# Row results in pieces of rows, and query weights transposed ahead, in a forward-and-backward decode block

## The chip, the cores and the metric

The kernel runs on one core of one Trainium2 chip. A core has a matrix engine (PE), a vector engine (DVE), an activation engine (ACT), a general engine (POOL) and a queue engine (SP) that only issues DMAs; 16 DMA engines move data between the device's memory and the core's on-chip memory (SBUF). PE writes to PSUM, from which DVE and ACT evict. The metric is the device time of one execution in microseconds, lower is better.

## The reference

The block is a sum of two branches on a normalised input, and the kernel computes its output and all gradients for one given `grad_out`:

```python
xn = layernorm(x)                                  # x: 2 x 1 x 576
# A: grouped-query attention on a cache
q = (xn @ wq)                                      # 32 heads of 128, 16 kv heads, 4096 cached rows
p = softmax(q k^T * 128 ** -0.5); o = p v
y = x + (o @ wo) + ((xn @ w_gate) * (xn @ w_up)) @ w_down     # F = 4608
out_0 = y
out_1 .. out_8 = gradients by x, k_cache, v_cache, wq, wo, w_gate, w_up, w_down
```

There are two rows (batch 2, one position each). The caches are 2 x 16 x 4096 x 128 in bf16, 33.6 MB each; their gradients, 33.6 MB each, are outer products of a vector over the cached rows and a vector over the 128 columns. All weights' gradients are outer products of rank two as well. So nearly all of the 186 MB that move are caches and weights read once and gradients written once. `out_0` and `out_1` are two rows of 576 values each. `out_1`, the gradient by x, is `grad_out` plus the layernorm's backward: (xn * mean(xn * g) − g + mean(g)) times −rstd, where g is the gradient by xn, added up over all groups and all MLP slices.

## The kernel before, in words

**Work.** The 16 kv heads are taken in eight groups of two, each for both rows of the batch: 16 steps `s`, group `s // 2`. A step loads two K and two V tiles of 1 MB (`load_kv`, L1132), turns each by two DVE transposes in 32 x 32 blocks (`turn`, L1207), scores on PE, softmax (`softmax`, L1316), the backward of it (`dscore`, L1372), two contractions with K and V (`contract`, L1423), and builds the four 1 MB gradient tiles by outer products on PE that ACT and DVE evict (`head_outer`, L1276, `unit`, L703) and SP stores (`put`, L696). The weights of a group are 0.5 MB of `wq` and 0.58 MB of `wo` (`load_w`, L1150). `group_front` (L982) computes q and the gradient by o; `group_back` (L1048) comes after both steps of a group: it adds the group's part of y to `acc` (L1082) and its part of the gradient by xn to `accx` (L1109), and starts the stores of the weights' gradients. The MLP is nine slices of 512 (`mlp`, L857), each of which adds to `acc` (L939) and `accx` (L971) too.

**Buffers.** All 1 MB tiles share 16 buffers `big` (L414): loaded K and V (`kv`, at most 6), turned tiles (`X`, at most 10), tiles to be stored (`st`, at most 5), gate and up weights (`G`). The weights of groups and slices share five buffers `ww`. For the part of the gradient by xn, `group_back` takes an `X` buffer, turns the group's `wq` into it by two DVE transposes (1.25 and 0.4 us in the planner's costs, L1098 and L1101), and only then gives the `ww` buffer back (L1099); then 32 products (`dxn`, L677) and the addition to `accx`.

**Order.** The engines' instruction streams are fixed when the program is built. Each piece of work is a generator that yields what it needs (an engine for so long, a buffer, an event); the class `Order` (L105) simulates these with its own costs and at each point gives an engine the piece of best priority among those that can start within `SLACK[engine]`. A priority is `STEP * s + PR[name]` plus tables by name and step (`pr`, L350; `OFF`, `HEAD`, `TAIL`); `WQ_AT`, `WO_AT`, `MLP_AT` say after how many K/V loads a weight's load may be issued. All large DMAs are issued by SP, in order; a DMA that waits for its buffer or its data holds up all that come after it on SP.

**Row results.** `consts` (L533) builds small masks. The last part of `front` (L641 to L668) makes x and the layernorm's values in columns: `xnT`, 128 partitions x 16. `acc` holds y as 5 chunks of 128 columns x 2 rows, on 128 partitions; `accx` holds the gradient by xn, folded over partitions, as 144 columns. At the end `final_out` (L1491) waits for all 17 additions to `acc`, turns it into two rows by nine fp32 products and adds x by two more products (`rows_add`, L1486), all into one PSUM tile of two partitions; ACT and DVE each evict a part (`rows_put`, L1478) and one DMA stores the row pair. `final_dx` (L1510) waits for the additions to `accx`, folds it by two products into 16 columns, computes the layernorm's backward in columns with eight small DVE operations and one product for the means, and turns the result into rows by eight fp32 products. In the order before it both have the same priority name, `fin`.

Of the kernel before, what the change touches and what calls it, by code (L numbers as in the profile page):

```python
# [13 lines left out]
P = 128  # L14
# [276 lines left out]
def DMA(engine, cost, nbytes, row=8192):  # L291
# [7 lines left out]
OFF = {"turn0": {0: 171.1, 1: 102.6, 2: -235.3, 3: 131.0, 4: -1229.9, 5: -180.7, 6: 339.1, 7: 83.9, 8: -1178.9, 9:  # L299
       1510.3, 10: 1749.8, 11: 637.8, 12: -214.3, 13: 330.3, 14: -900.9, 15: 113.0}, "turn1": {0: 455.2, 1: 413.9,  # L300
       2: 2138.7, 3: 65.8, 4: -397.2, 5: -528.4, 6: -1010.6, 7: -442.2, 8: -480.8, 9: -56.6, 10: 2098.4, 11: 87.0,
       12: -533.6, 13: -186.7, 14: 1823.6, 15: -1825.2}, "att": {0: -86.1, 1: 484.3, 2: 959.1, 3: 205.8, 4: -477.9,
       5: 588.8, 6: -2779.3, 7: -570.9, 8: 538.0, 9: -432.8, 10: -333.4, 11: 178.6, 12: 1763.9, 13: -38.0, 14: 9.3,
       15: -454.9}, "dsc": {0: -2.6, 1: -25.2, 2: 108.7, 4: -124.6, 5: 280.8, 6: -182.4, 7: 505.0, 8: 999.6, 10:
       1142.0, 12: -1624.8, 13: 450.2, 14: 26.1, 15: -1895.7}, "conv": {0: -1227.4, 1: -997.7, 2: -24.5, 3: 7.4, 4:
       -1788.1, 5: 528.6, 6: -1155.3, 7: -233.7, 8: -14.9, 9: 46.4, 10: -63.6, 11: -273.8, 12: -324.9, 13: -904.4,
       14: 156.5, 15: -1289.5}, "con": {0: 72.5, 1: 1065.5, 2: 2112.7, 3: 144.9, 4: 1119.6, 5: -318.8, 6: -807.3, 7:
# [4 lines left out]
       -906.9, 15: 763.8}, "front": {0: -1381.5, 1: -23.4, 2: -755.9, 3: 528.2, 4: 2459.1, 5: 22.3, 6: 15.4, 7:  # L312
       1614.9, 8: 1.0, 10: 390.9, 11: -4409.0, 12: 71.6, 13: -2214.6, 14: -86.2, 15: -206.6}, "back": {0: -538.7, 1:
# [7 lines left out]
       575.5, 9: -1893.1, 10: 29.8, 11: 1312.5, 12: -1551.8, 13: 2261.8, 14: -58.6, 15: -683.8}, "mlp": {0: 1005.2,  # L321
       1: -119.9, 2: 307.5, 4: -272.5, 5: -538.3, 6: -1285.0, 7: -2206.3, 8: -1506.9, 9: -1373.7, 10: -36.4, 11:
       -236.4, 12: 122.0, 13: 9.3, 14: -2474.7, 15: -1534.6}, "load": {0: 498.6, 1: 724.3, 2: -50.1, 3: 540.2, 4:
       106.4, 5: 1070.9, 6: -4.7, 7: -442.3, 8: 13.7, 9: -963.6, 10: -542.2, 11: -703.0, 12: -151.2, 13: 45.9, 14:
       -640.8}, "wload": {0: 155.4, 1: 205.4, 2: -85.0, 3: -865.8, 4: -2.0, 5: 2.5, 6: -0.9, 7: -303.6, 8: -1673.8,
       9: 962.0, 10: -188.9, 11: -608.2, 12: 86.0, 13: -143.2, 14: 1336.5, 15: 67.0}, "mload": {0: 43.2, 1: -50.8,
       2: 543.7, 3: -706.6, 4: -994.4, 6: -292.2, 8: 4096.0, 9: 58.8, 10: 972.1, 11: -299.2, 12: -233.4, 13: -24.9,
       14: 4269.4, 15: 2.2}}
MLP_AT = [0.0, 18.84, 14.07, 104.31, 26.44, 110.17, 0.0, 165.05, 136.25]
WQ_AT = [-187, 8, 14, 18, -93, -80, 45, 31]  # L330
WO_AT = [-23, -224, -88, -8, 34, 20, -51, -5]
# [3 lines left out]
BIAS = 0.255  # L335
SLACK = {"PE": 0.03, "ACT": 0.26, "DVE": 0.37, "POOL": 10000.0, "SP": 10000.0}
STEP = 28.0
HEAD = {"turn0": 81.5, "turn1": -4923.1, "att": -4504.9, "dsc": 207.7, "conv": -115.1, "con": 711.3, "out1":
        -3897.8, "out0": 1625.0, "front": 7985.6, "back": -1026.0, "W0": 2562.1, "W1": 3202.9, "BD1": -1330.7,
        "BD0": 7636.5, "mlp": 1972.6, "load": -4759.7, "wload": 3596.4, "mload": -2011.8}  # L340
TAIL = {"turn0": 4716.0, "turn1": 3086.8, "att": -169.4, "dsc": 2547.1, "conv": 1801.7, "con": 5805.3, "out1":
        12765.0, "out0": -437.4, "front": -225.5, "back": 3672.3, "W0": 3335.0, "W1": 3885.8, "BD1": -3217.7, "BD0":
        2296.5, "mlp": -2755.5, "load": -1393.2, "wload": 1480.7, "mload": -4914.1}
PR = {"turn0": 1153.7, "turn1": 1076.7, "att": -5721.2, "dsc": -1832.7, "conv": 859.0, "con": -1218.3, "out1":
      5153.5, "out0": 3270.3, "front": 245.1, "back": 420.1, "W0": -4343.9, "W1": 6157.7, "BD1": 4299.8, "BD0":
      -734.7, "mlp": -683.6, "wout": -1070.7, "store": 4212.6, "load": -375.6, "wload": -10719.3, "fin": 6841.0,
      "const": 8800.2, "mload": -3635.3}
# [8 lines left out]
def kernel(  # L356
# [121 lines left out]
    nmu = const.tile([2, 1], FP32, name="nmu")  # L478
    warm = const.tile([1, 1], FP32, name="warm")
    rstd = const.tile([2, 1], FP32, name="rstd")  # L480
# [9 lines left out]
    one1 = filled("one1", [1, 1], FP32, 1.0)  # L490
    ones = filled("ones", [P, 1], FP32, 1.0)
    meanc = filled("meanc", [P, 1], FP32, 1.0 / D)
    xnT = filled("xnT", [P, 16], FP32, 0.0)
    nrT = const.tile([P, 4], FP32, name="nrT")
    gg = const.tile([P, 2, 16], FP32, name="gg")
    gp4 = const.tile([P, 4], FP32, name="gp4")
    zero1 = filled("zero1", [P, 1], FP32, 0.0)
    acc = filled("acc", [P, 5, 2], FP32, 0.0)
# [104 lines left out]
    def front():  # L603
# [52 lines left out]
        for a in range(4):  # L656
            nc.tensor.matmul(tp[0:16, 8 + 2 * a:10 + 2 * a], lhsT=xb[:, 512 + 16 * a:528 + 16 * a],
                             rhs=ident[0:2, 0:2], start=True, stop=True)
# [932 lines left out]
```

## Time and profile before

| | |
|---|---|
| time, median of 3 runs | 467.26 us (466.91 to 468.17) |
| the profiled execution | 468.62 us, of which the span of its instructions 466.8 |
| moved | 185.87 MB in all packets; HBM read 92.48 MB, written 92.48 MB |
| mean rate over the span | 398 GB/s |
| busy | PE 78%, DVE 79%, ACT 70%, POOL 34% |
| mean granted PE clock | 0.72 of full |

The profile's page cuts the span into 40 slices of 11.7 us and gives each engine's busy share in tenths, the granted clock, the DMA engines' share and the rate. Its windows do the same for any stretch; a DMA share a little over 1 means that all sixteen are busy, since a packet's record overlaps the next by a few ns. Lists of waits say for which instruction of which engine an engine stood still, in total, how often and how long at most; `SPq` is SP's queue. The timeline lists instructions by start and duration, with the engine, the line, the operation and the tiles (`ps_m`, `ps_o` are PSUM tiles). fp32 products appear as pairs of instructions.

### The profile page before, as it was taken

Reading aid. Unit: us, or ns where it says so; the run is one execution under the profiler, and the core shown is the slowest. Engines: PE = TensorE matmul, PEld = TensorE weight load, DVE = VectorE, ACT = ScalarE, POOL = GpSimd, SP = SyncE. Lnnn points to the kernel's source line nnn. Section 1 sums busy time; section 2 is a strip of 40 time slices with the busy share of each in tenths; the row PEclk is TensorE's granted clock in tenths of the full one; section 3 lists DMA queues with packets and bytes.
Section 4 is the critical chain, followed back from the end, with each engine's and each line's share of the span. In section 5 each row is a group of like instructions: output and inputs, shape, how many; then the busy total and the mean of one; then the engine's idle time right before and its main releaser. Section 6 shows DMA issues by size and latency. Waiting matters only on the chain.

```text
span 466.8 us, 14164 instructions
## 1 busy us (share of the span) xinstructions
PE 364.8 (78%) x6001; PEld 203.9 (44%) x6002; DVE 370.5 (79%) x707; ACT 329.1 (70%) x478; POOL 160.7 (34%) x191
## 2 busy tenths in 40 slices
PE   1686857788887797878786689797987888798884
PEld 1543545454444334445353446443433454344452
DVE  8888789777889886869767789789885876888961
ACT  3268723767976678767885377589787887788981
POOL 0740113543105434553014654030515645063000
PEclk9999876767657758757875577769585657657875
DMA  8999999999999999999999999999999999999995
GB/s 314 413 409 415 418 423 394 401 386 343 400 417 411 410 412 372 420 423 422 421 415 412 414 406 413 397 367 364 418 423 426 422 426 423 384 350 416 421 380 221
DMA packets 39184, 185.87 MB, mean 398 GB/s; under 512 B 3336, under 2 KB 10448, under 8 KB 22736
## 3 DMA queue, kind: packets, MB, share of 16 engines
q1 hardware_dynamic: 39112, 184.96, 98.6%
q8 instruction: 47, 0.77, 0.6%
q14 instruction: 17, 0.14, 0.1%
q10 hardware_dynamic: 8, 0.00, 0.0%
HBM read 92.48 MB, written 92.48 MB: 396 GB/s over the span
## 4 chain that ended last, share of the span: by engine, by line
DMA 40%; PE 21%; ACT 11%; DVE 7%; issue 3%; POOL 1%; SPq 0%; ACTq 0%; DVEq 0%; POOLq 0%
DMA out_dram<-big 23%; DMA big<-in_A_v_cache_dram 14%; ACT big L471 9%; DVE big L467 5%; PE ps_o L1288 4%; PE ps_m L1440 3%; DMA ww<-in_B_w_down_dram 3%; PE ps_m L1266 2%; PE ps_o L732 2%; PE ps_m L896 1%; PE ps_m L1027 1%; PE ps_o L771 1%; POOL BD L1254 1%; DVE big L473 1%; PE ps_m L682 1%
## 5 line engine op out<-in xcount | busy, mean ns | idle before, releaser
L471 ACT CAST big<-ps_o 128x1024 bf16<-128x1024 f32 (+3 forms) x294 | 277.5, 1010 | 37.0 <-PE ps_o L1288 30.0
L467 DVE STREAM_TRANSPOSE big<-big 128x1024 f32<-128x1024 f32 x146 | 176.8, 1224 | 25.0 <-DMA big<-in_A_v_cache_dram 11.9
L1254 POOL TENSOR_TENSOR BD<-vr,mask 128x2048 bf16<-128x2048 bf16 x32 | 115.3, 3603 | 105.1 <-PE ps_o L1288 49.3
L473 DVE CAST big<-ps_o 128x1024 bf16<-128x1024 f32 (+2 forms) x79 | 82.5, 1048 | 11.1 <-PE ps_o L732 3.4
L1266 PE MATMUL ps_m<-big,W 128*32 128x128 bf16 x2048 | 56.9, 271 | 6.9 <-DVE hb L883 2.5
L1288 PE MATMUL ps_o<-BD,dd 32*128 32x512 bf16 x256 | 45.6, 471 | 14.4 <-ACT big L471 8.4
L1266 PEld LDWEIGHTS <-W 128*32 128x32 bf16 x2048 | 45.1, 120 | 23.7 <-issue 22.5
L1231 POOL COPY W<-rep 32x16 bf16<-32x16 bf16 x128 | 24.5, 192 | 78.5 <-DVE rep L1011 50.2
L1288 PE MATMUL ps_o<-BD,pp 32*128 32x512 bf16 x256 | 47.7, 504 | 4.4 <-ACT big L471 3.0
L467 DVE STREAM_TRANSPOSE big<-ww 128x1152 f32<-128x1152 f32 (+1 forms) x25 | 32.8, 1314 | 7.3 <-DMA out_dram<-big 2.9
L732 PE MATMUL ps_o<-dyr,RB 128*128 128x512 bf16 (+7 forms) x135 | 30.7, 370 | 4.0 <-ACT big L471 3.4
L1440 PE MATMUL ps_m<-big,pp 128*32 128x512 bf16 x256 | 30.9, 592 | 3.0 <-DVE pp L467 2.5
L742 POOL TENSOR_TENSOR RB<-R,maskq 128x512 bf16<-128x512 bf16 x8 | 8.3, 1042 | 58.9 <-ACT R L471 37.9
L1440 PE MATMUL ps_m<-big,dd 128*32 128x512 bf16 x256 | 25.6, 488 | 3.0 <-ACT big L471 1.7
L1288 PEld LDWEIGHTS <-dd 32*128 32x128 bf16 x256 | 11.3, 95 | 34.2 <-issue 27.3
L1288 PEld LDWEIGHTS <-pp 32*128 32x128 bf16 x256 | 10.8, 96 | 22.8 <-issue 19.0
L732 PEld LDWEIGHTS <-RB 128*128 128x128 bf16 x136 | 13.5, 119 | 13.7 <-issue 11.5
L1027 PE MATMUL ps_m<-big,Wdy 128*128 128x128 bf16 x144 | 14.6, 280 | 6.0 <-DVE Dm L902 3.0
L1027 PEld LDWEIGHTS <-Wdy 128*128 128x128 bf16 x144 | 13.3, 128 | 9.2 <-issue 6.8
L1341 ACT COPY sp<-m 1x128 f32<-1x128 f32 x16 | 4.7, 294 | 17.8 <-DVE m L1339 17.8
L896 PE MATMUL ps_m<-big,Wdy 128*128 128x128 bf16 x162 | 14.4, 258 | 3.4 <-DVE oT L1460 1.8
L471 ACT CAST osb<-ps_m 128x512 bf16<-128x512 f32 x15 | 8.8, 586 | 10.2 <-PE ps_m L1440 10.2
(205 smaller groups left out, 469.6 us busy)
## 6 DMA issues: line engine op xcount, KB each, us to landing
out_dram<-big SPq DMA_DIRECT2D x74, 1024.0 KB, 11.9
big<-in_A_k_cache_dram SPq DMA_DIRECT2D x32, 1024.0 KB, 12.6
big<-in_A_v_cache_dram SPq DMA_DIRECT2D x32, 1024.0 KB, 13.4
out_dram<-big SPq DMA_DIRECT2D x17, 576.0 KB, 10.6
ww<-in_B_w_down_dram SPq DMA_DIRECT2D x9, 576.0 KB, 13.3
ww<-in_A_wo_dram SPq DMA_DIRECT2D x8, 576.0 KB, 11.3
ww<-in_A_wq_dram SPq DMA_DIRECT2D x8, 512.0 KB, 11.8
big<-in_B_w_gate_dram SPq DMA_DIRECT2D x4, 1024.0 KB, 12.2
```

The source lines that it names most:

```text
L467: nc.vector.transpose(out, in_)
L471: nc.scalar.copy(out, in_)
L473: nc.vector.tensor_copy(out=out, in_=in_)
L732: nc.tensor.matmul(flat[:, x - lo:y - lo], lhsT=RB[:, c, :], rhs=dyr[:, n:n + y - x], start=True, stop=True)
L742: nc.gpsimd.tensor_tensor(RB[:].rearrange("p c (q m) -> p c q m", q=4), view(t, 0, P, 0, [[1, 4], [0, 4], [4, 32]]), view(maskq[:], 0, P, ...
L896: nc.tensor.matmul(dh, lhsT=Wdy[:, e, 2 * k:2 * k + P], rhs=view(X[:], 0, P, 64 * k + e, [[D, FC], [2, 32]]), start=(k == 0 and e == 0), s ...
L1027: nc.tensor.matmul(dp, lhsT=Wdy[:, e, 2 * k:2 * k + P], rhs=view(X[:], 0, P, 64 * k + e, [[D, GH], [2, 32]]), start=(k == 0 and e == 0), s ...
L1231: nc.gpsimd.tensor_copy(view(W_t[t][w][:], 32 * a, 32, 6 + 8 * a, [[G * WW, 4], [WW, G], [1, 2]]), view(rep_t[grp[g]["qs"]][:], 32 * a, 32 ...
L1254: nc.gpsimd.tensor_tensor(BD_t[i][:], view(vr_t[v][:], 0, P, 0, [[0, 16], [1, Dh]]), view(mask16[:], 0, P, 0, [[1, 16], [0, Dh]]), ALU.mult)
L1266: nc.tensor.matmul(sc[32 * cq:32 * cq + 32, :], lhsT=view(W[:], 0, P, (be * G + l) * WW + 6 - 4 * c2 - 2 * l, [[1, 32]]), rhs=view(X[:], 0 ...
L1288: nc.tensor.matmul(o[:, k, :], lhsT=pr2[32 * c4:32 * c4 + 32, :], rhs=BD[32 * c4:32 * c4 + 32, 8 * l + 4 * h2:8 * l + 4 * h2 + 4, :], star ...
L1440: nc.tensor.matmul(ct[32 * j:32 * j + 32, :], lhsT=view(rT, 0, P, 4 * c + 2 * l, [[1, 32]]), rhs=kv_t[kvS[s][t][l]][:, Dh * c:Dh * (c + 4) ...
```

## The change

- `out_0`: `acc` is laid out as 2 rows x 5 chunks, so that one fp32 product with the identity gives ten pieces of 128 columns on ten partitions. x has been brought to the same ten pieces early (`xrow`, in `front`); one DVE addition makes `yrow`, and four DMAs store the pieces.
- `out_1`: one product of `F8` with `accx` gives the gradient by xn as eight pieces of rows, 8 partitions x 144. The normalised x (`xn8`) and `grad_out` (`grow`) are in the same pieces since `front`. The sums are taken along the pieces on DVE, one small product with `M8` makes the two means for each piece, three DVE operations and a copy finish, and three DMAs store.
- Both now take a PSUM tile `m` where they took `o`; `out_0` has a priority name of its own, `finy`. The new values live in the tile `xy`, which grows from 2 to 10 partitions.
- The transposes of `wq` leave `group_back` for a stream of their own, `turn_wq`: for each group it waits for the group's `Ed` (the end of `group_front`) and for the spread of the softmax of its odd step, takes an `X` buffer, turns, gives the `ww` buffer back after the first transpose, and keeps the `X` buffer until `group_back` has used it.
- All numbers of the order (`OFF`, `HEAD`, `TAIL`, `PR`, `MLP_AT`, `WQ_AT`, `WO_AT`, `BIAS`, the slack of PE and DVE) are other ones, with entries for `finy` and `wqt`.

```diff
-SLACK = {"PE": 0.03, "ACT": 0.26, "DVE": 0.37, "POOL": 10000.0, "SP": 10000.0}
+SLACK = {"PE": 0.02, "ACT": 0.26, "DVE": 0.73, "POOL": 10000.0, "SP": 10000.0}
...
-MLP_AT = [0.0, 18.84, 14.07, 104.31, 26.44, 110.17, 0.0, 165.05, 136.25]
-WQ_AT = [-187, 8, 14, 18, -93, -80, 45, 31]
+MLP_AT = [2.39, 25.29, 14.72, 53.68, 27.42, 35.83, 0.0, 264.16, 163.71]
+WQ_AT = [-228, 8, -121, 19, -32, -129, 44, 46]
...
-        sums(F8[:], [[1, 8], [32, 4]])
+        sums(F8[:].rearrange("p (b a) -> p b a", b=2), [[1, 2], [2, 4], [32, 4]])
+        nc.vector.reduce_sum(K2[:], view(identf[:], 0, 8, 0, [[4, 2], [1, 4]]), axis=AX.X)
+        nc.vector.tensor_scalar(M8[:].rearrange("p (b a) -> p b a", b=2), view(K2[:], 0, 8, 0, [[1, 2], [0, 4]]), 1.0 / D, None, op0=ALU.mult)
+        nc.vector.tensor_copy(Z8[:].rearrange("p (b a) -> p b a", b=2), view(identf[:], 0, 2, 0, [[1, 2], [0, 4]]))
...
 (front, after the rows are normalised)
-        for a in range(4):
-            for c in range(4):
-                nc.tensor.matmul(tp[32 * c:32 * c + 32, 2 * a:2 * a + 2], lhsT=xb[:, P * c + 32 * a:P * c + 32 * a + 32],
-                                 rhs=ident[0:2, 0:2], start=True, stop=True)
...
+        for dc in range(5):
+            nc.tensor.matmul(tp[0:10, 288:416], lhsT=Zw[:, 4 - dc:14 - dc], rhs=xb[:, DOFF[dc]:DOFF[dc] + P],
+                             start=(dc == 0), stop=(dc == 4))
...
+        for n in range(2):
+            row = xy[0:2, n * D:(n + 1) * D]
+            for a in range(4):
+                nc.tensor.matmul(tp[0:8, 144 * n:144 * n + P], lhsT=Zw[:, 3 - a:11 - a],
+                                 rhs=view(row, 0, 2, 32 * a, [[P, 4], [1, 32]]), start=(a == 0), stop=(a == 3))
+            for a in range(4):
+                nc.tensor.matmul(tp[0:8, 144 * n + P:144 * n + 144], lhsT=Zw[:, 3 - a:11 - a],
+                                 rhs=row[:, 512 + 16 * a:528 + 16 * a], start=(a == 0), stop=(a == 3))
+        nc.tensor.matmul(tp[0:8, 416:418], lhsT=Z8[:], rhs=nmr[:], start=True, stop=True)
...
+    def turn_wq():
+        for g in range(NG):
+            st = grp[g]
+            yield PRIO(pr("wqt", 2 * g))
+            yield WAIT(st["Ed"], steps[2 * g + 1]["spread"])
+            wq = ww_t[st["wq"]]
+            x = st["wqt"] = yield ACQ("X")
+            X = X_t[x]
+            yield DVE(1.25)
+            t32(pairs(X[:, 0:4 * FS]), pairs(wq[:, 0:4 * FS]))
+            yield REL("ww", st["wq"])
+            yield DVE(0.4)
+            t32(pairs(X[:, 4 * FS:5 * FS]), pairs(tq[:, FS * (g % 4):FS * (g % 4 + 1)]))
+            yield SET(st["Ewqt"])
...
 (group_back; mlp likewise)
-        nc.vector.tensor_add(acc[:], acc[:], yp)
+        nc.vector.tensor_add(acc[:].rearrange("p b k -> p k b"), acc[:].rearrange("p b k -> p k b"), yp)
...
 (group_back)
-        x = yield ACQ("X")
+        yield WAIT(st["Ewqt"])
+        x = st["wqt"]
         X = X_t[x]
-        yield DVE(1.25)
-        t32(pairs(X[:, 0:4 * FS]), pairs(wq[:, 0:4 * FS]))
-        yield REL("ww", st["wq"])
-        yield DVE(0.4)
-        t32(pairs(X[:, 4 * FS:5 * FS]), pairs(tq[:, FS * (g % 4):FS * (g % 4 + 1)]))
...
+    def final_out():
+        yield PRIO(PR["finy"])
+        yield WAIT(Eprep, *acc_E)
+        i = yield ACQ("m")
+        yt = m_t[i][0:10, 0:P]
+        yield PE(0.0, 0.4)
+        nc.tensor.matmul(yt, lhsT=acc[:].rearrange("p b k -> p (b k)"), rhs=identf[:], start=True, stop=True)
+        yield DVE(0.25)
+        nc.vector.tensor_tensor(yrow, yt, xrow, ALU.add)
+        yield REL("m", i)
+        rows = out_0.rearrange("b s d -> (b s) d")
+        for b in range(2):
+            yield DMA("SP", 0.3, 1024, 256)
+            nc.sync.dma_start(rows[b, 0:512].rearrange("(c n) -> c n", c=4), yrow[5 * b:5 * b + 4, :])
+            yield DMA("SP", 0.3, 128, 128)
+            nc.sync.dma_start(rows[b:b + 1, 512:576], yrow[5 * b + 4:5 * b + 5, 64:P])
...
 (final_dx)
+        nc.tensor.matmul(g8, lhsT=F8[:], rhs=accx[:], start=True, stop=True)
+        yield DVE(0.6)
+        nc.vector.reduce_sum(s8[:, 0:1], g8, axis=AX.X)
+        nc.vector.tensor_tensor_reduce(out=t8, in0=xn8, in1=g8, scale=1.0, scalar=0.0, op0=ALU.mult, op1=ALU.add,
+                                       accum_out=s8[:, 1:2])
+        yield PE(0.0, 0.1)
+        nc.tensor.matmul(mt, lhsT=M8[:], rhs=s8, start=True, stop=True)
+        yield DVE(0.9)
+        nc.vector.tensor_copy(m8, mt)
+        nc.vector.scalar_tensor_tensor(out=t8, in0=xn8, scalar=m8[:, 1:2], in1=g8, op0=ALU.mult, op1=ALU.subtract)
+        nc.vector.tensor_scalar(t8, t8, m8[:, 0:1], nrs, op0=ALU.add, op1=ALU.mult)
+        nc.vector.tensor_tensor(dxrow, t8, grow, ALU.add)
+        yield REL("m", i)
+        rows = out_1.rearrange("b s d -> (b s) d")
+        for b in range(2):
+            yield DMA("SP", 0.3, 1024, 64)
+            nc.sync.dma_start(rows[b, 0:512].rearrange("(c a j) -> a c j", a=4, j=32),
+                              dxrow[4 * b:4 * b + 4, 0:P].rearrange("a (c j) -> a c j", j=32))
+        yield DMA("SP", 0.3, 256, 32)
+        nc.sync.dma_start(rows[:, 512:576].rearrange("b (a j) -> b a j", a=4), dxrow[0:8, P:144])
```

More of the change, by code (lines that the diff above doesn't have):

```diff
@@ L591, in front_y @@
         yield WAIT(Eiy)
-        yield from widen(xy[:, D:2 * D], dyr)
+        yield from widen(xy[0:2, D:2 * D], dyr)
         dyT = xnr[:].rearrange("p (k m) -> p k m", m=32)
@@ L659, in front @@
[L659 to L666 removed]
+        tp = m_t[i]
@@ L975, in mlp @@
         yield REL("hb", hs)
-    grp = [dict(Lm=Event(), Eq=Event(), Ed=Event(), Lo=Event(), EoT=Event()) for _ in range(NG)]
+    grp = [dict(Lm=Event(), Eq=Event(), Ed=Event(), Lo=Event(), EoT=Event(), Ewqt=Event()) for _ in range(NG)]
     Lq = events(2)
@@ L1476, in fronts @@
             yield from group_front(g)
-    def rows_put(o, n, out):
-        yield ACT(0.4)
-        nc.scalar.copy(view(xy[:], 0, 2, n * D, [[P, 5], [1, 64]]), o[0:2, 0, 0:320].rearrange("p (k n) -> p k n", k=5))
-        yield DVE(0.4)
-        nc.vector.tensor_copy(view(xy[:], 0, 2, n * D + 64, [[P, 4], [1, 64]]), o[0:2, 1, 0:256].rearrange("p (k n) -> p k n", k=4))
-        yield DMA("SP", 0.3, 2304, 1152)
-        nc.sync.dma_start(out.rearrange("b s d -> (b s) d"), xy[:, n * D:(n + 1) * D])
-    def rows_add(o, n):
-        for k in range(2):
-            nc.tensor.matmul(o[0:2, k, 0:320 - 64 * k], lhsT=ident[0:2, 0:2],
-                             rhs=view(xy[:], 0, 2, n * D + 64 * k, [[P, 5 - k], [1, 64]]), start=True, stop=False)
     def final_out():
-        yield PRIO(PR["fin"])
+        yield PRIO(PR["finy"])
         yield WAIT(Eprep, *acc_E)
-        i = yield ACQ("o")
-        o = o_t[i]
-        yield PE(1.1, 0.5)
-        rows_add(o, 0)
-        for dc in range(5):
-            r = slice(0, P) if dc < 4 else slice(64, P)
-            for k in range(2):
-                if dc < 4:
-                    nc.tensor.matmul(o[0:2, k, 64 * dc:64 * dc + 64], lhsT=acc[:, dc, :],
-                                     rhs=identf[:, 64 * k:64 * k + 64], start=False, stop=(dc == 3 and k == 1))
-            if dc == 4:
-                nc.tensor.matmul(o[0:2, 0, 256:320], lhsT=acc[64:P, 4, :], rhs=identf[64:P, 64:P],
-                                 start=False, stop=True)
-        yield from rows_put(o, 0, out_0)
-        yield REL("o", i)
+        i = yield ACQ("m")
[11 more added lines that the diff above has]
+            nc.sync.dma_start(rows[b:b + 1, 512:576], yrow[5 * b + 4:5 * b + 5, 64:P])
     def final_dx():
@@ L1525, in final_dx @@
-        nc.vector.tensor_tensor(gx, g, xnT[:], ALU.mult)
-        nc.vector.reduce_sum(gp4[:], view(gg[:], 0, P, 0, [[16, 2], [1, 2], [2, 8]]), axis=AX.X)
-        yield PE(0.0, 0.1)
-        nc.tensor.matmul(mt[:, 16:20], lhsT=view(meanc[:], 0, P, 0, [[0, P]]), rhs=gp4[:], start=True, stop=True)
-        yield DVE(0.5)
-        mean = [view(mt[:], 0, P, 16 + 2 * k, [[0, 8], [1, 2]]) for k in range(2)]
-        nc.vector.tensor_tensor(gx, xnT[:], mean[1], ALU.mult)
-        nc.vector.tensor_tensor(gx, g, gx, ALU.subtract)
```

164 lines of the change are left out of this document (73 added, 91 removed), and 22 rows, old and new, of the table OFF.

## The prediction

> **What bounds the kernel now.** I read the page's slices first, then the DMA queues, then DMA by stretches of 10 us, then what SP waited for in the weak stretches, and last the tail instruction by instruction.
>
> ```profile
> DMA  8999999999999999999999999999999999999995
> GB/s 314 413 409 415 418 423 394 401 386 343 400 417 411 410 412 372 420 423 422 421 415 412 414 406 413 397 367 364 418 423 426 422 426 423 384 350 416 421 380 221
> ...
> q1 hardware_dynamic: 39112, 184.96, 98.6%
> q8 instruction: 47, 0.77, 0.6%
> ```
>
> The DMA engines are busy all the time; no compute engine is (DVE 79%, PE 78%). What varies is the rate: some 420 GB/s in most slices, 343 to 372 in a few. Those and the two ends are all that an order of the work can win; the bytes stay as they are. The windows of 10 us give the weak stretches (last columns: granted clock, DMA share, GB/s):
>
> ```profile
> 300.00:310.00 10.00, 7.62 (x142) 4.71 (x140) 7.83 (x19) 6.86 (x12) 4.60 (x2) 0.67 0.94 347
> 320.00:330.00 10.00, 7.17 (x159) 3.37 (x147) 9.36 (x14) 8.11 (x11) 1.56 (x1) 0.88 0.99 364
> 410.00:420.00 10.00, 9.69 (x139) 4.46 (x139) 8.72 (x13) 8.79 (x11) 7.16 (x2) 0.51 1.01 350
> ```
>
> Priced as (420 − rate)/420 x 10 us: 300 to 310 lost 1.7 us, 320 to 330 1.3, 400 to 420 2.9 (369 and 350), 90 to 120 4.0 (372, 369 and 353). What stood before two of them is in SP's waits (total, times, longest) of 290 to 306 and of 314 to 326, and in the timeline:
>
> ```profile
> SPq L1163 <- PE ps_m L935: 8.1, 1, 8.1
> SPq L1163 <- DVE big L467: 1.8, 1, 1.8
> 324.22 1.20 DVE L467 STREAM_TRANSPOSE big<-ww 128x1024 f32<-128x1024 f32 x1
> 325.44 0.38 SPq L1163 DMA_DIRECT2D ww<-in_A_wq_dram  x1
> ```
>
> L1163 is the load of a group's query weights. SP, which issues in order, stood 8.1 us before it for one of the five weight buffers (`ww`), and at 305 to 306 the packets took only 0.62 of the DMA engines' time. The second time it went on 0.02 us after group 4's transpose of query weights had ended (324.22 + 1.20 = 325.42), the instruction that frees the buffer.
>
> The tail:
>
> ```profile
> 453.81 1.87 PE L1502 MATMUL ps_o<-identf,acc 128*2 128x64 f32 x16
> 455.91 0.59 PE L1519 MATMUL ps_m<-F,accx 128*128 128x8 f32 x2
> 457.15 0.61 PE L1288 MATMUL ps_o<-BD,pp 32*128 32x512 bf16 x2
> 457.80 1.01 ACT L471 CAST big<-ps_o 128x1024 bf16<-128x1024 f32 x1 [1.36 <-PE ps_o L1288]
> 458.84 0.36 SPq L700 DMA_DIRECT2D out_dram<-big  x1
> 459.16 1.87 PE L1538 MATMUL ps_o<-identf,gg 128*2 128x128 f32 x8 [0.89 <-DVE gg L1534]
> 461.81 0.26 SPq L1484 DMA_DIRECT2D out_dram<-xy  x1
> ```
>
> The rows' fp32 products (L1502, L1519) stand on PE ahead of the last pair of the last big store (L1288), so that store is issued at 458.84, and `out_1` at 461.81. But the row isn't what ends the span. In windows of 1 us:
>
> ```profile
> 458.00:459.00 1.00, 0.28 (x2) 0.19 (x1) 0.58 (x4) 0.81 (x1) 0.00 (x0) 0.50 0.48 192
> 463.00:464.00 1.00, 0.00 (x0) 0.00 (x0) 0.00 (x0) 0.00 (x0) 0.00 (x0) 0.50 0.06 25
> 464.00:465.00 1.00, 0.00 (x0) 0.00 (x0) 0.00 (x0) 0.00 (x0) 0.00 (x0) 0.50 0.08 33
> ```
>
> A share of 0.06 is one engine of sixteen. The trace's packets say the same: 14 of the last store's 16 completions come at 462.2 to 462.4, the row's two packets at 462.5 and 462.6, and one engine alone goes on with eight packets of 8 KB, 0.31 us each, to 465.3. Going back, that engine has packet after packet through 458 to 460 too, while the others are dry. It runs behind by what it has done more (the 47 instruction fetches of 16 KB take 0.98 us each, on one engine at a time): of the store issued at 452.38 the middle completion is at 456.3, the last at 460.8.
>
> **The change part by part.**
>
> Setup. About eleven DVE instructions on constants and on x in columns (L489 to L494, L645 to L666; rows 0.07 to 0.22 us, one 0.50) give way to about as many on `Zw`, `Z8`, `M8`, `K2` and the pieces, and 21 small products to 22. Between −0.3 and +0.6 us of DVE, taken at 0: at 10 to 20 us DVE works 7.9 of 10 us and DMA moves 426 GB/s from loads that were issued before. Were that cover gone, its ends would count.
>
> `out_0`. Gone from PE: L1488 0.64, L1502 1.87, L1505 0.37, together 2.9 us; in comes one fp32 product of 128 columns, by L1538 (four in 1.87) 0.47. Two evictions of 0.41 become one DVE addition, by L1531 0.2. One DMA becomes four: at 0.26 to 0.32 each (L1484) SP spends 0.9 us more. `acc` is added to with its two axes exchanged, same ten columns (L1082, 0.15): 0 to +0.03 each, taken at 0, since DVE isn't what DMA waits for here.
>
> `out_1`. Before, 455.91 to 461.81 is 5.9 us. After: product of 144 columns 0.53, sum 0.2, product-and-sum 0.33 (L1384 0.25 and 0.08), second product 0.3 (L1528 is 0.59 at 128 rows; here 8), four small DVE operations 0.8, waits between engines 0.3: 2.5 us, then three issues, 0.9. So the row is ready some 2.5 us earlier, and the last pair of L1288 no longer queues behind 2.4 us of PE: the last big store could be issued up to 2.4 us sooner. SP has seven row DMAs instead of two; the last store, if queued behind the four of `out_0`, gives back 0.9 of that.
>
> What this does to the end: the 15 engines lose their hole at 458.3 to 459.7 (1.2 us by the shares 0.48 and 0.44), the sixteenth has no hole to lose. So 0 at least, −1.2 at most, where no engine is far behind. I take −0.4, nearer to 0 because the late engine is in the trace.
>
> Query weights ahead. The 1.20 and 0.42 us of DVE per group are the same eight times, only sooner: from after the odd step's spread. In between lie, by the starts of the rows `pp<-sp` and `big<-ww`, 30, 39, 23, 35, 43, 32, 19 and 23 us, 245 in all. By up to that much one of 5 weight buffers is free sooner, and one of 16 big buffers is held longer. On DVE, K and V transposes queue behind each pair for 1.6 us; DMA's queue covers that (a load lands 12 to 13 us after its issue). Both SP waits above should go: group 3's pair could run from 216 instead of 250, group 4's from 281 instead of 324. Worth 1.7 + 1.3 = 3.0 us at most. At least 0, if the late engine decides: at 303 to 306 it wasn't dry (the store issued at 296.89: middle completion 306.3, last 310.8), and of the load issued at 305.92 it was 2.7 behind instead of 4.5, so the others' hole was in part only its catching up. I take −1.6, the middle, because after such a hole all engines are slow (packets of 8 KB at over 0.6 us at 323, against 0.31).
>
> The order. All priorities are new; what gates the weights' loads (`WQ_AT`, `MLP_AT`) moves by a few issues. It can close the stretches of 90 to 120 and 400 to 420 (−6.9) or open others of that size. No row shows which; taken at 0, with 4 us to each side (the 90 to 120 stretch) for the range.
>
> Sum: −0.4 − 1.6 = −2.0. The profiled execution took 468.62 (span 466.8 and 1.8 around it), so 466.6 for one like it; it stands 1.36 over the median 467.26, so **465.3**.
>
> **The rivals.**
>
> *Nothing gained, 467.3 (465.9 to 468.6).* The late engine sets the end, and holes of the others are its slack. For: 465.3 is its last packet, 3 us after the rest. Against: it too loses in the slow packets after a hole. This holds too if `wqt`'s priorities put the transposes no earlier than now: then only the tail's 0 to 1.2 is left.
>
> *Buffers run short, 471 (468.7 to 475).* The transposed weights hold a big buffer for 245 us more, 3.3% of 16 x 467; a K or V load then waits on SP for a store to land, and everything behind it in SP's order waits too. For: L1141 already waited 19.8 us for stores' landings. Against: 13 times, 2.5 at the longest. It decides once such a wait passes some 6 to 8 us (the 8.1 us wait emptied the queue). One stretch like 90 to 120 costs 4.0: 467.3 + 4.0 = 471.3. An order that is worse in another place would look the same in GB/s.
>
> *The rows land last, 468.5.* The 50 pieces (256, 128, 64 and 32 bytes) queue on a few engines, and if one of these is the late one, behind its 465.3. At 0.05 us a piece (a 1152-byte packet) 16 on one engine take 0.8 us, and issue to landing 0.9 as for `out_1` now. Against: with the last eviction at 458.8 as now the row would be out at 458.8 + 2.5 + 0.9 + 0.9 = 463.1; the chain must start 2 us later to decide. The Trainium skill ("DMA: Bandwidth & Descriptors", Specifications) has pieces under 512 bytes read, changed and written back; taken as twice 0.05 the 16 pieces would be 1.6 us, an estimate from that page, and the rival 469.3. No row here shows such a piece but the completions of 4 bytes, 9 ns.
>
> **How the numbers follow.** Forecast 0.48 (its own range 460.5 to 465.8), nothing gained 0.15, buffers short or a worse order 0.33, rows last 0.04. About 0.3%, 1.4 us, is what a measurement here tells from no change. So faster 0.48, same 0.19, slower 0.33. Below 461 I leave some 0.07 (it needs two of the four weak stretches gone), above 471.5 some 0.12.
>
> **What would show it.** Right: no wait of L1163 or L1196 over 2 us, no slice under 380 between 290 and 330; L1288's last pair not behind fp32 products; the last row's issue within 4 us of the last addition to `accx`. Right on the late engine: a share near 0.06 for some us at the end although the last store is issued sooner. Wrong: longer waits at L1141 for landings, slices under 360 in new places, or a last landing that is a row's.

## The result, and the profile after

The changed kernel takes 473.09 us (median of 6 runs, 469.85 to 474.23), the kernel before 467.08 beside it (6 runs, 466.67 to 468.17). The ratio is 1.0114, interval 1.0079 to 1.0148: slower by 1.1%, 6.0 us, where 465.3 was forecast and the range ended at 471.5.

The profiled execution after took 471.04 us (span 469.3), 2.05 under its median; that of before took 1.5 more than its own. So these two traces are 2.5 us of span apart and show the kind of the loss, not all of its size. The page of the changed kernel:

```profile
DMA  8999999999999999999999899999999999999996
GB/s 303 412 409 388 398 421 408 401 424 400 423 416 405 354 415 410 421 422 421 395 398 423 346 400 399 377 416 398 417 376 380 423 423 406 404 423 402 414 334 235
...
q1 hardware_dynamic: 39174, 184.96, 98.5%
q8 instruction: 46, 0.75, 0.6%
```

DMA still bounds it, and the compute engines have as much to do as before (PE 76%, DVE 78%). The weak slices of before (343 at 105 to 117, 367 and 364 at 303 to 327, 350 at 408 to 420) are at 398 to 423 now. But there are new ones of 354, 346, 377, 376 and 380, and the end is 334 and 235 instead of 380 and 221. Windows of 10 us on the new weak places (last columns: granted clock, DMA share, GB/s):

```profile
150.00:160.00 10.00, 6.70 (x100) 4.29 (x102) 9.93 (x16) 4.55 (x8) 7.57 (x7) 0.50 0.97 354
260.00:270.00 10.00, 7.24 (x104) 5.64 (x107) 7.34 (x10) 2.83 (x6) 7.93 (x4) 0.50 0.86 335
350.00:360.00 10.00, 8.54 (x140) 5.11 (x139) 7.03 (x14) 8.34 (x16) 1.04 (x1) 0.84 1.00 354
450.00:460.00 10.00, 8.85 (x177) 5.22 (x176) 6.74 (x13) 8.01 (x12) 1.04 (x1) 0.67 0.90 325
```

SP's waits over the whole execution (total, times, longest; L1167 is now the load of K and V, L1189 that of `wq`):

```profile
SPq L1167 <- DMA out_dram<-big: 17.3, 10, 6.3
...
SPq L1167 <- DVE big L471: 7.9, 2, 7.5
...
SPq L1189 <- PE ps_m L950: 6.7, 2, 4.4
...
SPq L1189 <- DVE big L477: 4.5, 1, 4.5
```

The 8.1 us wait for a `ww` buffer is gone, though SP still stood 4.4 and 4.5 us before loads of `wq`. But a K or V load now stood 6.3 us for the landing of a store (2.5 at the longest before; in total such waits are no longer, 17.3 us against 19.8), and another one 7.5 us behind DVE. That second one is the hole at 260 to 270; the timeline shows what came first:

```profile
257.77 2.37 DVE L471 STREAM_TRANSPOSE big<-big 128x1024 f32<-128x1024 f32 x2 [2.38 <-DMA out_dram<-big]
...
260.25 1.38 DVE L471 STREAM_TRANSPOSE big<-ww 128x1152 f32<-128x1152 f32 x1
261.68 2.08 PE L1042 MATMUL ps_m<-big,Wdy 128*128 128x128 bf16 x18 [6.13 <-DVE big L471]
...
263.79 0.45 ACT L475 CAST dof<-ps_m 128x128 bf16<-128x128 f32 x1 [7.89 <-PE ps_m L1042]
...
265.10 2.33 DVE L471 STREAM_TRANSPOSE big<-big 128x1024 f32<-128x1024 f32 x2
...
267.36 1.27 SPq L1167 DMA_DIRECT2D big<-in_A_v_cache_dram  x2
```

DVE stands 2.38 us in its queue because the buffer that it is to write still waits for a store's landing. Behind it PE is idle for 6.13 us, ACT for 7.89, and SP, which needs what they free, issues nothing between 255.8 and 267.36. That is a cost of buffers, of the kind that my rival "Buffers run short" describes. The tail:

```profile
455.98 0.60 PE L1510 MATMUL ps_m<-identf,acc 128*10 128x128 f32 x2
457.03 0.27 DVE L1512 TENSOR_TENSOR xy<-ps_m,xy 10x128 bf16<-10x128 f32 x1
457.32 0.34 SPq L1517 DMA_DIRECT2D out_dram<-xy  x1
457.71 0.32 SPq L1519 DMA_DIRECT2D out_dram<-xy  x1
458.13 0.36 SPq L715 DMA_DIRECT2D out_dram<-big  x1
...
458.95 0.29 DVE L1135 TENSOR_TENSOR accx<-accx,ps_m 128x144 f32<-128x144 f32 x1
459.39 3.98 SPq L715 DMA_DIRECT2D out_dram<-big  x3
...
460.86 0.65 PE L1527 MATMUL ps_m<-accx,F 128*8 128x144 f32 x2
...
463.30 0.29 DVE L1538 TENSOR_TENSOR xy<-xy 8x144 bf16<-8x144 f32 x1
463.62 1.32 SPq L1543 DMA_DIRECT2D out_dram<-xy  x2
465.46 0.71 SPq L1546 DMA_DIRECT2D out_dram<-xy  x1
```

The rows are as short as forecast (0.6 us of PE for `out_0` instead of 2.9; 2.7 us from 460.86 to the finished row). Yet the last big store, the third of those from 459.39, is issued at 463.0, later than in before (458.84). And again one DMA engine goes on alone after the others, in windows of 1 us:

```profile
464.00:465.00 1.00, 0.00 (x0) 0.00 (x0) 0.00 (x0) 0.00 (x0) 0.00 (x0) 0.50 1.00 404
...
466.00:467.00 1.00, 0.00 (x0) 0.00 (x0) 0.00 (x0) 0.00 (x0) 0.00 (x0) 0.50 0.07 25
467.00:468.00 1.00, 0.00 (x0) 0.00 (x0) 0.00 (x0) 0.00 (x0) 0.00 (x0) 0.50 0.06 23
```

### The profile page after: what moved, and what is told of

The parts are those of the page before. It is cut to its first block, busy times and chain, and to the rows that moved or that the text cites. A ratio compares the mean times of both kernels' runs of the same rounds, so it can differ in the third digit from the quotient of the medians.

```text
span 469.3 us, 14112 instructions
## 1 busy us (share of the span) xinstructions
PE 357.0 (76%) x5963; PEld 201.5 (43%) x5965; DVE 365.9 (78%) x702; ACT 332.4 (71%) x480; POOL 160.4 (34%) x191
## 4 chain that ended last, share of the span: by engine, by line
PE 33%; DMA 25%; DVE 20%; ACT 13%; issue 6%; POOL 2%; ACTq 0%; DVEq 0%; SPq 0%; POOLq 0%
DMA out_dram<-big 15%; DVE big L471 11%; ACT big L475 10%; PE ps_m L1466 6%; PE ps_m L1292 6%; PE ps_o L1314 6%; DMA big<-in_A_v_cache_dram 5%; DMA big<-in_A_k_cache_dram 3%; PE ps_m L1042 3%; DVE big L477 2%; PE ps_o L747 2%; POOL BD L1280 2%; PE ps_m L911 1%; PE ps_m L697 1%; PE ps_m L893 1%
## 5 line engine op out<-in xcount | busy, mean ns | idle before, releaser
L471 DVE STREAM_TRANSPOSE big<-big 128x1024 f32<-128x1024 f32 x146 | 176.6, 1224 | 19.8 <-DMA out_dram<-big 8.9
L477 DVE CAST big<-ps_o 128x1024 bf16<-128x1024 f32 (+2 forms) x75 | 77.1, 1031 | 23.2 <-PE ps_o L747 7.9
L1292 PE MATMUL ps_m<-big,W 128*32 128x128 bf16 x2048 | 59.3, 281 | 3.1 <-issue 1.8
L1292 PEld LDWEIGHTS <-W 128*32 128x32 bf16 x2048 | 48.3, 126 | 23.3 <-issue 21.6
L1466 PE MATMUL ps_m<-big,dd 128*32 128x512 bf16 x256 | 30.4, 568 | 5.9 <-DVE dd L471 2.9
L747 PE MATMUL ps_o<-dyr,RB 128*128 128x512 bf16 (+7 forms) x134 | 28.1, 351 | 5.5 <-DVE big L477 2.3
L1466 PE MATMUL ps_m<-big,pp 128*32 128x512 bf16 x256 | 29.1, 552 | 3.3 <-DVE pp L471 2.1
L1042 PE MATMUL ps_m<-big,Wdy 128*128 128x128 bf16 x144 | 14.5, 279 | 7.2 <-DVE big L471 6.5
L786 PE MATMUL ps_o<-Dm,xnr 32*128 32x512 bf16 x64 | 12.6, 521 | 8.7 <-ACT big L475 7.3
L1476 ACT ACTIVATE osb<-ps_m 128x512 bf16<-128x512 f32 x13 | 7.9, 607 | 10.3 <-PE ps_m L1466 4.6
```

The lines of the kernel that those rows point to most:

```text
L471: nc.vector.transpose(out, in_)
L477: nc.vector.tensor_copy(out=out, in_=in_)
L747: nc.tensor.matmul(flat[:, x - lo:y - lo], lhsT=RB[:, c, :], rhs=dyr[:, n:n + y - x], start=True, stop=True)
L786: nc.tensor.matmul(o[:, aa, 0:n * P], lhsT=xnr[32 * a:32 * a + 32, dc * P:(dc + 1) * P], rhs=rhs(a), start=True, stop=True)
L1042: nc.tensor.matmul(dp, lhsT=Wdy[:, e, 2 * k:2 * k + P], rhs=view(X[:], 0, P, 64 * k + e, [[D, GH], [2, 32]]), start=(k == 0 and e == 0), s ...
L1292: nc.tensor.matmul(sc[32 * cq:32 * cq + 32, :], lhsT=view(W[:], 0, P, (be * G + l) * WW + 6 - 4 * c2 - 2 * l, [[1, 32]]), rhs=view(X[:], 0 ...
```

## The experiments

The change has three parts that the planner couples: with another piece of work or another number, it orders everything anew. To try a part alone, the planner's decisions were recorded (4218 for before: which piece comes next, on which engine, in which buffer) and the program lays the pieces in that sequence. Pieces that the part adds are put in as soon as they can start.

```diff
+PICKS = (
...
     def run(self):
-        while self.streams:
...
+        for n, (name, k, e, slot) in enumerate(picks):
+            s = find(name, k)
...
+                    ok = self.step(s, e, slot)
```

**The parts alone in before's order, and the old rows in the new order.** e1 has the row results of the change and `wq` as in before; e2 has `wq` ahead and the old rows; e3 both. e4 holds the order of the changed kernel, keeps `wq` ahead and puts the old rows in.

> The order of before is held piece by piece on every engine and buffer; only the row results are computed as in the changed kernel (pieces of rows, seven row DMAs behind the same stores). If the order is what costs (theory 1): 465.5 to 468.0 us, the tail's 0 to 1.2 us at most to be won, since one DMA engine is late. If the row edit itself costs (theory 2: seven row DMAs and DVE work at the end): 469 or more, with the last store's issue later than 458.8.

> The order of before is held; only the transposes of the query weights stand ahead, right behind the odd step's spread, and the buffers of the weights are picked anew. Theory 1 (order): 465 to 468, the waits of SP for a weight buffer at 297 and 323 gone. Theory 2 (the big buffer held longer runs the loads short): 469.5 or more, with longer waits of the K and V loads (the line that issues them).

> Both edits in the order of before. Theory 1 (order): 464.5 to 468, so that the changed kernel's 473.1 less this is what its order costs, 5 to 8 us. Theory 2 (edits): 471 to 474.

> The changed kernel in its own order, held piece by piece, with the row results computed as in before (two row DMAs). Theory 1 (order): 471 to 474.5, like the changed kernel. Theory 2 (the rows): 467 to 469.

Measured, as ratios to before: e1 469.93 us, 1.0069 (1.0049 to 1.0089). e2 529.67, 1.1347 (1.1313 to 1.1381). e3 532.21, 1.1397 (1.1351 to 1.1443). e4 474.21, 1.0142 (1.0110 to 1.0173).

Only e4 lands in theory 1's band. e1 and e2 land in theory 2's, e2 some 60 us above its lower end, and e3 in neither. So the rows alone cost 2.9 us, `wq` ahead costs 62 us in an order that was not made for it, and in the new order it makes no difference which rows are in (the changed kernel stood at 1.0114). For e1 the timeline of the start shows where:

```profile
16.55 1.04 PE L1446 MATMUL ps_m<-big,W 128*32 128x128 bf16 x32 [0.53 <-ACT dof L640]
...
17.53 0.69 PE L826 MATMUL ps_m<-xy,Zw 2*10 2x128 bf16 x5
18.28 0.06 DVE L829 MEMSET Zw<- 2x7 uint32 x1 [0.83 <-PE ps_m L826]
...
18.59 0.58 PE L835 MATMUL ps_m<-xy,Zw 2*8 2x128 bf16 x4 [0.37 <-DVE Zw L830]
...
20.93 0.26 PE L1218 MATMUL ps_m<-ident,dof 128*128 128x128 bf16 x1 [1.10 <-DVE xy L846]
21.13 1.04 PE L1446 MATMUL ps_m<-big,W 128*32 128x128 bf16 x32
```

The two lines at L1446 are the first two scores. Between them the new setup goes from DVE to PE and back three times, and PE, which works in order, waits each time. In before the second score starts at 18.05, here at 21.13. What follows is about 3 us late: the first store is issued at 34.04 instead of 31.25, and the 20th megabyte has moved 2.1 us later. The lines of before for the second score and the first stores, and then that of e1 for the first stores:

```profile
18.05 1.04 PE L1266 MATMUL ps_m<-big,W 128*32 128x128 bf16 x32
31.25 4.28 SPq L700 DMA_DIRECT2D out_dram<-big  x2
```

```profile
34.04 5.05 SPq L880 DMA_DIRECT2D out_dram<-big  x2
```

**The setup put elsewhere, and the row DMAs behind the last store.** e5 is e1 with the setup's last part held back to the middle (to the 1109th piece, and then to places where PE is busy); e6 also holds the four DMAs of `out_0` until the last big store is issued; e7 has the changed kernel's order, with its setup moved in the same way.

```diff
 (e5, then e6)
+LATE, HELD, PATIENT, MARGIN = {'front': 1109}, {}, {'front': 'PE'}, 0.3
+LATE, HELD, PATIENT, MARGIN = {'front': 1109}, {'final_out': 4213}, {'front': 'PE'}, 0.3
...
+            if name in LATE and const and n < LATE[name]:
+                return False
+            if name in HELD and s.req[0] == "dma" and n < HELD[name]:
+                return False
```

> Before's order held piece by piece, the row results alone, as in e1, but the three setup products and their DVE pieces (Zw, M8, xrow, grow, xn8) stand some 130 us later, between pieces whose engines are busy, instead of between the first and the second score. Theory A (e1 lost its time at the start: the second score 3.1 us late, the first store issued at 34.04 instead of 31.25, and about 1 us more at the tail): the first store is issued at 31.0 to 31.6 and the time falls from e1's 469.9 to 467.3 to 468.5. Rival B (this order has no slack at all, and the setup costs its length wherever it stands): 469.3 to 470.8, with the lag over before appearing at 130 to 145 us instead of at 17 to 21. Rival C (e1's loss is all at the tail): first store as in A, time 469.3 to 470.5.

> e5 with the four row DMAs of out_0 put behind the last big store on SP; nothing else differs. Theory A (SP's four row DMAs delayed the last store by 1.9 us in e1): the last big store is issued at most 0.5 us later than in before, 0.5 to 1.2 us under e5, so 466.6 to 467.6. Rival D (the late DMA engine, not the last store's issue, sets the end): within 0.4 us of e5. Rival E (seven row DMAs in one queue at the end cost more than they free): 0.5 to 1.5 us over e5.

> The changed kernel with its own order held, the setup products and their DVE pieces alone moved from 12 to 16 us to some 150 us. Theory A (the first store 2.7 us late is never made up): first store issued at 31.0 to 32.0, time 470.2 to 471.7 against the changed kernel's 473.1. Rival F (later waits in this order, such as the chain at 255 to 267, swallow what the start gains): first store early, time 472.3 to 474. Rival B (costs its length wherever it stands): 472.5 to 474 with the lag over the changed kernel beginning at 150 us.

e5: 468.04 us, ratio 0.9999 (0.9977 to 1.0021). Theory A holds: the first store is issued at 30.28, even sooner than A said, and the whole loss of e1 is gone. e6: 468.53, 1.0018 (0.9994 to 1.0042). That is 0.5 us over e5, at the edge between rivals D and E, which the intervals don't tell apart; theory A falls, so holding the row DMAs back gains nothing. In e5's trace the last big store is issued at 457.23, 1.6 us sooner than in before, and the rest of the tail shows what that is worth, in windows of 1 us:

```profile
460.00:461.00 1.00, 0.00 (x0) 0.00 (x0) 0.00 (x0) 0.00 (x0) 0.00 (x0) 0.50 0.59 232
461.00:462.00 1.00, 0.00 (x0) 0.00 (x0) 0.00 (x0) 0.00 (x0) 0.00 (x0) 0.50 0.06 25
462.00:463.00 1.00, 0.00 (x0) 0.00 (x0) 0.00 (x0) 0.00 (x0) 0.00 (x0) 0.50 0.08 33
```

Fifteen engines are done at 460.8 (462.4 in before), one goes on to 463.6 (465.3). This execution was 1.3 us under e5's median; over all runs the gain isn't there.

e7: 471.61 us, 1.0100 (1.0059 to 1.0141). The time lies within theory A's band, but its sign does not come: the first store moves only from 33.93 to 33.32. The interval holds the changed kernel's 1.0114. The first scores do come sooner (16.06 instead of 17.49), but the first store hardly does, and in e4, the same order with before's rows and setup, it is issued at 34.33. So in that order the late first store is the order's own and not the new setup's. What the setup costs there in all isn't resolved; by these figures it isn't most of the 6 us.

**The big buffer of the transposed `wq`.** e8 is e2 with a later start; e9 turns `wq` inside its own `ww` buffer at the early place; e10 does so at the old place.

```diff
 (e8: turn_wq)
-            yield WAIT(st["Ed"], steps[2 * g + 1]["spread"])
+            yield WAIT(st["Ed"], *steps[2 * g]["done"], *steps[2 * g + 1]["done"])
 (e9: turn_wq; e10: group_back)
-            t32(pairs(X[:, 0:4 * FS]), pairs(wq[:, 0:4 * FS]))
+            t32(pairs(wq[:, 0:4 * FS]), pairs(wq[:, 0:4 * FS]))
```

> Before's order and rows, with the transposes of wq ahead of group_back by 5 to 10 us only (they wait for the group's both steps, and take a big buffer that has been free for 2 us by the planner's clock), instead of right behind the odd step's spread as in e2. Theory H (e2's 62.6 us come from the big buffer that the transposed wq holds for 25 us and more, so that DVE waits for landings of stores in the order held): loses a small part of that, 468 to 478. Rival I (any second big buffer at that place breaks an order that has none to spare): 490 to 530. The term of my prediction alone (a ww buffer free earlier, SP's waits at the wq loads gone): 464.3 to 466.5.

> Before's order and rows; wq is transposed ahead at the same early places as in e2 and in the changed kernel (right behind the odd step's spread), but inside its own ww buffer, so that it takes no big buffer; its tail goes through Xt inside group_back, and the ww buffer stays taken until the group's dx products. A load that finds no ww buffer slips behind the next pieces. Theory H (the big buffer held for 21 to 63 us a group is what cost e2 62.6 us and e8 30 us): 467 to 473, and no DVE wait for a store's landing over 5 us. Rival J (DVE's 1.25 us pieces at the early places break the order held, buffer or not): 490 to 530.

> Control for e9: before's order and rows, wq transposed inside its own ww buffer at the old place in group_back, so the 33 us in all for which before's eight groups hold a big buffer for it are saved, and ww buffers stay taken 2 to 8 us longer each. Theory H: within 1.5 us of before (466.5 to 469), since the order held cannot use the buffer any sooner. Rival K (a ww buffer freed later delays the weight loads, SP's waits at them grow): 469 to 473.

e8: 498.37 us, 1.0648 (1.0613 to 1.0684). e9: 469.80, 1.0048 (1.0030 to 1.0067). e10: 468.50, 1.0014 (0.9990 to 1.0038). From each trace, the time from the first transpose of a group's `wq` to the end of the group's last dx product, summed over the eight groups, is 33 us in before, 313 in e2, 104 in e8. DVE's waits for landings go with it; here are those of e2, of e8, of e9 and of before:

```profile
DVE big L635 <- DMA out_dram<-big: 55.3, 10, 9.7
```

```profile
DVE big L656 <- DMA out_dram<-big: 34.6, 9, 10.1
DVE big L662 <- DMA out_dram<-big: 13.8, 2, 12.5
```

```profile
DVE big L678 <- DMA out_dram<-big: 10.6, 10, 3.2
```

```profile
DVE big L467 <- DMA out_dram<-big: 12.0, 9, 3.4
```

So theory H holds for e2: with the same early DVE pieces and no big buffer, 60 of the 62 us are gone, and rival J falls. e8 fits rival I rather than H's band: holds of 4 to 24 us are enough to break an order in which no buffer is to spare. e10, the control, is within theory H's band. e9 keeps 2.2 us; whether that is the early pieces or the `ww` buffers kept longer was not told apart.

**Orders found anew.** The changed kernel's own order, though, holds big buffers for the transposed `wq` for 201 us (14 to 32 a group) at a cost of 6 us, not 62. So I let the planner find orders: its tables were moved in small steps from before's, and each step was kept if the planner's own clock put the end sooner.

```diff
 (e11, some of its tables)
-MLP_AT = [0.0, 18.84, 14.07, 104.31, 26.44, 110.17, 0.0, 165.05, 136.25]
-WQ_AT = [-187, 8, 14, 18, -93, -80, 45, 31]
+MLP_AT = [-0.51, 24.91, 14.07, 96.06, 26.44, 113.51, 15.7, 141.78, 165.21]
+WQ_AT = [-197.85, 8, 14.12, 21.99, -94.96, -63.45, 45.09, 46.26]
 (e13 and e14: in front)
+        yield WAIT(Econst, Emore, steps[3]["sm"])
 (e15, all of it)
-BIAS = 0.255
+BIAS = 0.28
```

> The row results alone, wq as in before, with an order found anew: the planner's tables moved step by step from before's, 988 tries. Theory L (the changed kernel's loss comes with wq ahead and its buffer hold, and the row results can be planned around): 466.5 to 469.5, first store issued before 32 us. Rival M (any order found anew for the row results costs 3 us and more, as the changed kernel's did): 470.5 to 476.

> Rows and wq ahead, as in the changed kernel, with another order, found from the same start in the same time as e11's. Theory L (wq ahead leaves the planner fewer big buffers, so that no order found for it comes back to before's time): 471 to 476, 3 us and more over e11, and each group's transposed wq again holds its buffer for over 10 us. Rival M (the order found for the changed kernel was an unlucky one): 466.5 to 469.5, no different from e11.

e11 (rows, `wq` as before): 474.40 us, 1.0141 (1.0102 to 1.0181). e12 (rows and `wq` ahead): 474.19, 1.0135 (1.0089 to 1.0182). The big buffers are held for 26 us in all in e11 and 203 in e12, and the times are the same. Theory L falls. In both traces the 20th megabyte is 3 us and more late (3.6 and 3.1; 2.1 in e1), so the setup at the start could still have been the cause; the next three were to tell.

> As e11 (row results alone, wq as in before, order found anew in 1890 tries), but the setup products must wait for the softmax of the fourth step, so that they cannot stand at the start. Theory N (e11's loss was the setup at the start, 3.6 us at 20 MB, and what the search then could not mend): 465 to 469, first store issued before 32 us. Rival M (any order found anew by this planner costs 3 us and more on the chip, since its clock is not the chip's): 470 to 476.

> As e13, with wq ahead as in the changed kernel; order found from the same start in 1902 tries. Theory L (wq ahead leaves too few big buffers in any order): 3 us and more over e13. Rival M (the order, not wq ahead): within 2 us of e13.

> Before's code without any part of the change; one number of the planner is moved (BIAS, by which it weighs the engines that may evict, from 0.255 to 0.28), so that the same work comes in another order. Theory M (an order that the tables were not made for costs as much as the changed kernel lost): 471 to 478. Rival: the order's term stays within the 4 us of my prediction: 466 to 471.

e13: 474.59 us, 1.0151 (1.0110 to 1.0193). e14: 474.90, 1.0143 (1.0095 to 1.0191). e15: 476.77, 1.0200 (1.0159 to 1.0240). Rival M has it three times. With the setup away from the start (first store at 29.92 and 29.60) the orders found are no better, and the 20th megabyte is 3.0 and 2.6 us late all the same; `wq` ahead (187 us of holding in e14, 33 in e13) again changes nothing that shows, though e11 to e14 each have an order of their own, so that a difference of `wq` ahead and one of the order could offset each other. And before's own code loses 2.0% when one number of the planner moves by a tenth. The rates of e13, then of e15:

```profile
GB/s 308 414 408 353 380 423 329 394 417 414 421 411 419 417 417 386 417 413 414 383 391 421 411 411 390 363 363 378 419 419 421 424 424 425 419 402 352 413 238 320
```

```profile
GB/s 316 413 410 412 421 416 395 412 384 356 413 417 405 402 379 415 413 418 421 416 416 414 404 289 399 379 423 418 425 424 424 423 424 424 412 411 286 291 309 177
```

e13 has weak slices at 35 to 47, 71 to 83 and near the end. e15 has moved 170 MB at 421.1 us, 1.4 sooner than before, and loses all of its 9.6 us after that. The slice at 35 to 47 is weak in all four orders found anew (317, 328, 353 and 383 GB/s in e11 to e14, 415 in before) but not in e15 (412); otherwise the weak places differ, and no one wait was found to explain all five.

The planner's clock can be set beside the chip. The last DMA of e11 and e13 is issued, by that clock, 0.8 us after and 1.5 us before that of before. But an execution ends with the last landing, and by the landing of the last DMA that `Order` works out while the program is built, every one of these orders comes after before's:

| | planner's clock, last landing, us | chip, median, us |
|---|---|---|
| before | 467.1 | 467.1 |
| changed kernel | 473.5 | 473.1 |
| e11 | 471.7 | 474.4 |
| e12 | 478.5 | 474.2 |
| e13 | 469.0 | 474.6 |
| e14 | 475.9 | 474.9 |
| e15 | 478.0 | 476.8 |

So the clock has the sign right six times of six, and the changed kernel's and e15's sizes to within 1.5 us. It misses most of e13's loss (2.0 of 7.4 us) and it puts `wq` ahead some 7 us behind (e12 after e11, e14 after e13), which the chip doesn't show. That its figure for the changed kernel is so close may be luck.

## Why the prediction was wrong, point by point

- **"The order. … taken at 0", with 4 us to each side.** This is the step that failed. Five orders that are not before's took 474.2 to 476.8 us with five different sets of work, and the changed kernel 473.1: +6 to +10 us each, none at 0 and none below. e15 has before's own work, so the order alone is enough for a loss of this size. I treated the order as a term whose sign is unknown, since no row of the profile shows it. But before's order was the special one of the set: a 10% move of one number was enough to lose 2%. And the sign was to be had without the chip: the planner's own clock lands the changed kernel's last DMA 6.4 us after before's. What isn't shown is the changed kernel's own case through and through: no run held its order with `wq` turned in `group_back` as before, so how much of its 6.0 us goes with the held buffers stays open.
- **"Setup. … taken at 0", covered by loads issued before.** Wrong in before's order: 2.9 us in e1, nothing in e5 with the same pieces elsewhere. The eleven DVE operations and the products had the right size. The cover was wrong: the loads in flight did keep DMA busy until 30 us, but the scores that lead to the first store stood behind three trips between PE and DVE, and in e1 DMA was short of work later, at 38 to 47 us (329 GB/s against 409 in before).
- **"Query weights ahead", −1.6.** Not seen in any pair: e12 against e11 and e14 against e13 differ by under 0.1% of 474. The mechanism was half right. SP's 8.1 us wait did go, but the sign that I had named, no wait over 2 us at the loads of `wq` and `w_down`, didn't come (4.4, 4.5 and 4.0 us), and waits of 6.3 and 7.5 us at the K/V loads came, which I had priced only in the rival. In before's order the buffer, not the DVE time, costs 60 us (e2 against e9).
- **The tail, −0.4 (0 to −1.2).** e5, all of the rows' change without the setup's place, stands at 0.9999, −1.1 to +1.0 us, so the term is within its bounds and not shown to gain. The last big store was issued 1.6 us sooner than in before in e5's trace, but 4.2 later in the changed kernel's, whose order puts other pieces before it. The last row was issued 6.2 us after the last addition to `accx`, where I had named 4 as the sign. The late engine is there in every tail shown. "Three issues, 0.9" was too little: the `out_1` DMAs held SP from 463.62 to 466.17, 2.6 us (0.28, 0.98 and 0.71 us, the rest waits). The 0.98 isn't the price of its 16 small pieces, for the same DMA took 0.27 in e5.
- **"The rows land last"**, 0.04: not what happened; the last packets are again those of one late engine with 4.6 KB packets, to 467.9, the rows' last pieces at 466.8. There I had cited the Trainium skill ("DMA: Bandwidth & Descriptors", Specifications): pieces under 512 bytes are read, changed and written back. The packets here took 18 ns (256 bytes), 10.5 (64) and 8.3 (32), so no such price shows in the packets, and the estimate of 0.1 us a piece is far off.
- **"Buffers run short, 471", 0.33.** Its signs came as listed: longer waits for landings, slices under 360 in new places. By the time alone it was the right case. As the cause it isn't shown: e13 holds as few big buffers as before and loses as much. What the changed kernel has is its other half, "an order that is worse in another place", and that was worth more than I gave it.

What stays open: what in before's order suits the chip. The planner's clock sees a part of it only (2.0 us of e13's 7.4), and most of the weak places differ from order to order. Nor do the two traces hold all of the 6.0 us.

## What to carry to other kernels

Where a kernel's order was searched for, a change to its work and a new order are two changes; hold the old order piece by piece and measure the edit in it, or the edit's own worth (here 0 for the rows, once the setup stood off the first store's path) can't be told from the order's. If a planner has a clock, ask it for the last landing before a forecast is made: here it gave the sign of the loss. But an order that it found must still be measured on the chip: e13, 2.0 us after before by the clock, came 7.4 us after it. And setup work is free only if it isn't queued, on an in-order engine, ahead of the first thing that feeds the bound resource.

## What was not expected of the hardware

- **Full and yet slow.** Stretches with a DMA share of 1.0 moved as little as 350 to 367 GB/s. In them it is the 8 KB packets that take longer: 370 ns on average at 350 to 360 in the changed kernel, 356 at 290 to 300, against 312 at 410 to 420, where the rate is 425. In before it is 385 at 320 to 330. Share alone doesn't tell a good stretch; no run here tells why the packets are slow.
- **Late completions grow through the execution.** A store or load has sixteen completions, and in e5 the last comes 1.4 us after the middle one between 20 and 120 us, but 4.6 between 360 and 460 (medians). Its store issued at 451.72 has the middle one at 455.0 and the last at 459.1, one issued at 444.62 448.95 and 453.7. In the end one engine is behind and adds 2 to 3 us with a share of 0.06. The instruction fetches (46 packets of 16 KB in the changed kernel, 962 ns each, never two at a time) add to one engine's work; that they cause the lag was not tried. The Trainium skill ("Runtime: NRT & Kernel Launch", Instruction fetch mechanics) calls the cost of such a refill mostly hidden; for the fetching engine it may be, but here all sixteen DMA engines are the bound.
- **A small DMA may wait for an old big one.** In e1 the third DMA of `out_1` stood 2.2 us on SP for the landing of a store, though its data was ready; all three went at 461.21, 462.59 and 465.04, just after the last completion of the store issued eight DMAs earlier (461.15, 462.57 and 465.02). That they waited for that store's completion lane is inferred from this and the program, not tried.
